# Bucketed attention and a snake MLP on one core: first batch pair by pair, alpha folded into the weights, one form of mask rows

## The chip, the cores and the metric

The kernel runs on 1 core of one Trainium2 chip. The metric is device time in microseconds (us) of one execution. A run is listed as slow when it is more than 1.5% above the fastest of the same kernel, and as fast otherwise. A ratio in this text is the mean time of one kernel's fast runs over the mean of the other's fast runs of the same rounds, so it is not quite the ratio of the medians that stand beside it. The rounds ran on different chips of the same kind; where kernels of different rounds are compared, the ratios are the safer figures.

Engines: PE multiplies matrices (PEld is its loading of weights), DVE and ACT work on vectors, POOL is the general engine, SP issues most of the DMA transfers.

## The reference, cut to what matters

```python
# q, k, v: (4, 8, 768, 64) = batch, heads, positions, head size; proj: (64, 6)
q_bits = (q @ proj > 0); k_bits = (k @ proj > 0)         # 6 bits: a bucket number
mask   = q_bucket[..., :, None] == k_bucket[..., None, :]
scores = where(mask, q @ k.T / 8, -1e9)
attn   = softmax(scores) @ v                             # -> x: (3072, 512)
h = x @ w_in                                             # expand: 512 -> 2048
s = sin(alpha * h)
g = h + s * s / (alpha + 1e-9)
out = g @ w_out                                          # contract: 2048 -> 512
```

## The kernel before

The kernel plans its own order. Every piece of work is an operation with an engine, an assumed duration, dependencies, a priority and buffers; a list scheduler in Python runs once while the kernel is built and fixes the order of each engine. On the chip every engine then runs its own list strictly in order. An assumed duration that is wrong therefore costs a wait, not a new order.

The unit of attention is one pair of heads, one half (384 positions) of the queries: 6 score steps, each followed by an exponential, sums for the denominator, the product with v, ln and exp for the reciprocal. One batch has 8 units.

```python
# the mask: rows of +-32 below the 64 rows of q and k make non-matching buckets vanish in the exponential
NROW = 2 * NB; KR = D + 2 * NROW                          # 64 + 24 = 88 rows
nc.vector.tensor_scalar(out=bits[:, 0, :],      in0=z, ..., op0=ALU.is_gt, op1=ALU.mult)
nc.vector.tensor_scalar(out=bits[64:128, 1, :], in0=z[64:128], ...)          # a second form for k
# 4 row transfers for each pair, 24 rows each
# [cut]
# weights straight from HBM to bf16 by the transfer
nc.gpsimd.dma_start(out=win[p][:, cs], in_=moe_w_in[128*p:128*p+128, cs])
# [cut] expand: two 384-wide Sin with a per-partition scale, two 384-wide fused adds
for i in range(2):
    nc.scalar.activation(out=s[:, i, :], in_=two(hh, "pair")[i][:, 0:HS], func=AF.Sin, scale=alpha[:, 2*s_+i:2*s_+i+1])
for i in range(2):
    nc.vector.scalar_tensor_tensor(out=g[:, F, :], in0=s2[:, i, :], scalar=inva[:, F:F+1],
                                   in1=two(hh, "pair")[i][:, 0:HS], op0=ALU.mult, op1=ALU.add)
# [cut] batch 0 in two groups: the first halves of all four pairs, expand, the second halves, expand
groups = [(0, [(p, 0) for p in range(NPAIR)], [0]), (0, [(p, 1) for p in range(NPAIR)], [1])]
groups += [(b, [(p, c) for p in range(NPAIR) for c in range(2)], [0, 1]) for b in range(1, B)]
```

The contraction of one group is what fills PE during the attention of the next group.

The softmax here doesn't subtract the row's maximum and nothing guards it: scores larger than these inputs give would overflow.

## Time and profile before

| | before |
|---|---|
| median (fast runs) | 381.2 us |
| span in the profile | 379.2 us |
| first score | 18.0 us |
| attention of batch 0 / its expand phases | 36 + 27 us / 14 + 19 us |
| attention of batches 1, 2, 3 | 55, 55, 45 us |
| expand phases of batches 1, 2 | 28, 29 us |

Two lines of the page of the kernel before: PE's busy time with its share of the span, and the clock that PE was granted in 40 equal slices of the span (in tenths of full speed, 9 is 90% or more).

```profile
PE 327.4 (86%) x1914; PEld 153.9 (41%) x1936; DVE 285.7 (75%) x494; ACT 280.3 (74%) x430; POOL 79.7 (21%) x107
...
PEclk9996799699999999699999999999999999999899
```

The windows view of the kernel before, cut at the loads of ACT's function table, which part attention (exponentials) from expand phases (Sin): start and end, length, then the busy time of each engine with its number of instructions, the granted clock, the busy share of DMA and GB/s.

```profile
core 0: us, PE busy (x) PEld busy (x) DVE busy (x) ACT busy (x) POOL busy (x), PEclk, DMA share, GB/s
0.00:18.00 18.00, 10.37 (x63) 6.58 (x64) 10.67 (x49) 3.43 (x4) 8.56 (x21) 1.00 0.91 219
18.00:53.90 35.90, 28.37 (x171) 11.72 (x171) 25.07 (x46) 26.93 (x42) 15.14 (x25) 0.86 0.98 155
53.90:68.30 14.40, 10.98 (x65) 6.20 (x64) 13.31 (x23) 14.12 (x23) 3.70 (x4) 1.00 0.22 35
68.30:95.00 26.70, 25.56 (x146) 10.30 (x148) 20.45 (x32) 22.33 (x34) 5.29 (x6) 0.87 0.46 76
95.00:113.60 18.60, 16.48 (x98) 8.42 (x101) 16.06 (x28) 13.78 (x21) 5.42 (x6) 1.00 0.20 42
113.60:168.20 54.60, 47.42 (x280) 19.88 (x283) 44.05 (x65) 44.12 (x67) 13.95 (x15) 0.94 0.53 90
168.20:196.30 28.10, 24.11 (x146) 13.03 (x146) 26.29 (x46) 24.82 (x42) 5.42 (x6) 1.00 0.19 30
196.30:251.30 55.00, 50.22 (x309) 22.15 (x314) 43.14 (x62) 44.01 (x65) 13.70 (x15) 1.00 0.52 94
251.30:280.50 29.20, 26.28 (x156) 14.48 (x157) 28.61 (x51) 24.13 (x41) 4.17 (x5) 1.00 0.15 30
280.50:325.90 45.40, 44.76 (x278) 19.74 (x282) 31.10 (x54) 39.45 (x61) 4.35 (x4) 1.00 0.22 54
325.90:379.20 53.30, 42.87 (x216) 21.43 (x215) 26.93 (x49) 23.13 (x40) 0.00 (x0) 0.97 0.09 32
```

The second line is the first four units of batch 0, the third an expand phase, and so on in turn; the last is batch 3's expand and the final contraction. PE is nearly full in batch 3's attention (44.76 of 45.40 us), which has no next batch to prepare. Expand phases have DVE busy for 86% to 98% of the time (the last line, which holds the contraction too, aside). DMA is full until 54 us.

Groups of instructions of the kernel before (line, engine, operation, shapes, count, busy us, mean ns, then idle time before them):

```profile
L467 DVE TENSOR_TENSOR sum<-sum,E 128x768 bf16<-128x768 bf16 x64 | 40.1, 626 | 5.3 <-ACT E L457 1.5
L543 ACT ACTIVATE s<-pp,alpha 128x384 bf16<-128x384 f32 x108 | 55.6, 579 | 13.6 <-PE pp L537 13.3
L559 DVE SCALAR_TENSOR_TENSOR g<-s,inva,pp 128x384 bf16<-128x384 bf16 x108 | 59.8, 606 | 1.1 <-ACT s L550 0.2
```

The first line is a group of the adds for the denominators. One step of an expand phase took two Sin of 579 ns on ACT and two adds of 606 ns on DVE.

### The profile page before, as it was taken

The page shows a single profiled execution, that of the slowest core. Times are in us where ns is not written, and L with a number is a line of the kernel's source. Part 1 is how long each engine was busy: PE and PEld are TensorE (multiplying, and loading weights), DVE is VectorE, ACT ScalarE, POOL GpSimd, SP SyncE. Part 2 cuts the span into 40 slices and gives each one's busy share as a digit, 9 for nine tenths or more (in the row PEclk, how much of TensorE's full clock was granted, in tenths as well). Part 3 has the DMA queues.
Part 4 walks back from the last instruction along what each step waited for, and adds up shares of the span by engine and source line. Part 5 has one row for each costly group of instructions (what it writes and reads, how often), then busy time and mean ns, then how long its engine had stood idle before and what let it go on. Part 6 is the DMA issues. An engine that isn't in the chain of part 4 may idle for free.

```text
span 379.2 us, 5493 instructions
## 1 busy us (share of the span) xinstructions
PE 327.4 (86%) x1914; PEld 153.9 (41%) x1936; DVE 285.7 (75%) x494; ACT 280.3 (74%) x430; POOL 79.7 (21%) x107
## 2 busy tenths in 40 slices
PE   3787787899799997787899889997999999897895
PEld 3442244243354332244444333443544344454342
DVE  4797479679895888978977987899986956599121
ACT  1357899798778888599799784898789899798000
POOL 5475210204500315402300540332000300000000
PEclk9996799699999999699999999999999999999899
DMA  8859990155306277351033724651024101100022
GB/s 208 208 81 182 214 148 14 21 91 101 75 7 112 66 110 116 53 98 24 0 59 69 131 51 73 136 111 21 17 51 89 45 3 45 40 0 0 2 83 83
DMA packets 94859, 28.80 MB, mean 76 GB/s; under 512 B 79664, under 2 KB 90736, under 8 KB 94832
## 3 DMA queue, kind: packets, MB, share of 16 engines
q1 hardware_dynamic: 86560, 21.11, 26.8%
q0 software_dynamic: 7680, 7.34, 13.0%
q8 instruction: 15, 0.25, 0.3%
q10 hardware_dynamic: 592, 0.00, 0.1%
q14 instruction: 12, 0.10, 0.1%
HBM read 27.27 MB, written 6.29 MB: 89 GB/s over the span
## 4 chain that ended last, share of the span: by engine, by line
PE 47%; DVE 23%; ACT 12%; DMA 7%; issue 7%; SPq 3%; DVEq 0%
PE pb L580 16%; PE pp L453 10%; PE pp L537 10%; PE pp L491 7%; DVE g L559 5%; ACT E L457 5%; DVE sum L467 5%; DVE F L337 3%; DMA tok<-in_k_dram 3%; DVE s L552 3%; ACT s L543 2%; DMA tok<-in_q_dram 2%; DMA QK<-bits 2%; SPq L327 2%; PE pb L355 2%
## 5 line engine op out<-in xcount | busy, mean ns | idle before, releaser
L457 ACT ACTIVATE E<-pp 128x768 bf16<-128x768 f32 x192 | 148.9, 812 | 28.1 <-PE pp L453 27.1
L453 PE MATMUL pp<-QK 88*128 88x384 bf16 x384 | 92.3, 341 | 12.2 <-ACT E L457 8.0
L580 PE MATMUL pb<-wout,g 128*128 128x512 bf16 x362 | 96.0, 386 | 7.6 <-DVE g L559 3.4
L398 POOL CAST QK<-F 64x768 bf16<-64x768 f32 (+1 forms) x63 | 53.9, 860 | 205.4 <-DVE F L337 194.1
L537 PE MATMUL pp<-xt,win 128*128 128x384 bf16 x432 | 74.6, 326 | 10.4 <-DVE g L559 9.5
L537 PEld LDWEIGHTS <-win 128*128 128x128 bf16 x512 | 49.8, 98 | 49.1 <-issue 16.3
L467 DVE TENSOR_TENSOR sum<-E 128x768 bf16<-128x768 bf16 x64 | 38.3, 604 | 37.5 <-ACT E L457 37.3
L543 ACT ACTIVATE s<-pp,alpha 128x384 bf16<-128x384 f32 x108 | 55.6, 579 | 13.6 <-PE pp L537 13.3
L559 DVE SCALAR_TENSOR_TENSOR g<-s,inva,pp 128x384 bf16<-128x384 bf16 x108 | 59.8, 606 | 1.1 <-ACT s L550 0.2
L453 PEld LDWEIGHTS <-QK 88*128 88x128 bf16 x384 | 33.0, 100 | 64.5 <-issue 41.0
L580 PEld LDWEIGHTS <-g 128*128 128x128 bf16 x384 | 37.0, 99 | 49.7 <-issue 16.4
L491 PE MATMUL pp<-E,V 128*64 128x385 bf16 x384 | 46.3, 350 | 4.3 <-DVE xt L510 3.7
L467 DVE TENSOR_TENSOR sum<-sum,E 128x768 bf16<-128x768 bf16 x64 | 40.1, 626 | 5.3 <-ACT E L457 1.5
L337 DVE STREAM_TRANSPOSE F<-tok 128x768 f32<-128x768 f32 x24 | 37.7, 1572 | 1.3 <-DMA tok<-in_q_dram 1.2
L591 DVE COPY osb<-pb 128x512 f32<-128x512 f32 x20 | 13.7, 688 | 25.1 <-PE pb L580 25.0
L491 PEld LDWEIGHTS <-V 128*64 128x64 bf16 x384 | 17.6, 112 | 31.1 <-issue 26.9
L552 DVE TENSOR_TENSOR s<-s 128x768 bf16<-128x768 bf16 x40 | 22.3, 567 | 6.4 <-ACT s L543 6.2
L504 ACT ACTIVATE ln<-pp,epsb 128x384 f32<-128x384 f32 x32 | 18.6, 582 | 11.0 <-PE pp L496 10.5
L510 DVE SCALAR_TENSOR_TENSOR xt<-pp,ln 128x384 bf16<-128x384 f32 x32 | 19.7, 616 | 1.5 <-ACT ln L507 1.3
L467 DVE TENSOR_TENSOR sum<-sum 128x768 bf16<-128x768 bf16 x32 | 20.3, 633 | 0.7
L550 ACT ACTIVATE s<-s 128x768 bf16<-128x768 bf16 x22 | 18.4, 843 | 0.6
L507 ACT ACTIVATE ln<-ln 128x384 f32<-128x384 f32 x32 | 16.8, 523 | 0.0
(49 smaller groups left out, 185.2 us busy)
## 6 DMA issues: line engine op xcount, KB each, us to landing
out_dram<-osb SPq DMA_DIRECT2D x24, 256.0 KB
tok<-in_q_dram SPq DMA_DIRECT2D x48, 96.0 KB
tok<-in_k_dram SPq DMA_DIRECT2D x48, 96.0 KB
V<-in_v_dram POOLq DMA_DIRECT2D x16, 192.0 KB, 3.8
QK<-bits SPq DMA_DIRECT2D x60, 36.0 KB
win<-in_moe_w_in_dram POOLq DMA_DIRECT2D x8, 256.0 KB, 7.3
wout<-in_moe_w_out_dram POOLq DMA_DIRECT2D x8, 256.0 KB, 12.2
tok<-in_q_dram SPq DMA_DIRECT2D x4, 384.0 KB
```

The source lines that it names most:

```text
L337: nc.vector.transpose(out=fh[0].slots["F"][:, ti, :].rearrange("p (j i a) -> p a j i", j=NJ, a=4), in_=hold_t.slots["tok"].rearrange("p (t ...
L398: nc.gpsimd.tensor_copy(out=d_, in_=s_)
L453: nc.tensor.matmul(out=o.slots["pair"][:, h, 0:HS], lhsT=qk[0:KR, 1, h, 128 * j:128 * j + 128], rhs=qk[0:KR, 0, h, c * HS:(c + 1) * HS], s ...
L457: ex = P.op("ACT", 0.695, lambda o, e, sc=sc, j=j: nc.scalar.activation(out=eh.slots["E"][:, j, :, 0:HS], in_=sc.slots["pair"][:, :, 0:HS] ...
L467: o = P.op("DVE", 0.47, lambda o, e: nc.vector.tensor_tensor(out=dst(), in0=a(), in1=b_(), op=ALU.add), deps=deps + [sh], prio=10 + ui * 1 ...
L491: nc.tensor.matmul(out=nd[D * h:D * h + D, 0, 0:HS + 1], lhsT=vt[:, h, jmap(b, j), :], rhs=et[:, j, h, 0:HS + 1], start=(j == 0), stop=(j ...
L510: xe = P.op("DVE", 0.6, lambda o, e: nc.vector.scalar_tensor_tensor(out=xt_hold[(b, c)].slots["xt"][:, p, :], in0=v0.slots["nd"][:, 0, 0:H ...
L537: nc.tensor.matmul(out=two(o, "pair")[i][:, 0:HS], lhsT=win[p][:, 128 * F:128 * F + 128], rhs=xt[:, p, :], start=(p == 0), stop=(p == NPT ...
L543: nc.scalar.activation(out=o.slots["s"][:, i, :], in_=two(hh, "pair")[i][:, 0:HS], func=AF.Sin, scale=alpha[:, 2 * s_ + i:2 * s_ + i + 1])
L552: (nc.gpsimd if e == "POOL" else nc.vector).tensor_tensor(out=o.slots["s2"], in0=x, in1=x, op=ALU.mult)
L559: nc.vector.scalar_tensor_tensor(out=gh.slots["g"][:, F, :], in0=sq.slots["s2"][:, i, :], scalar=inva[:, F:F + 1], in1=two(hh, "pair")[i][ ...
L580: nc.tensor.matmul(out=acc, lhsT=g_hold[(b, c)].slots["g"][:, F, 128 * tb:128 * tb + 128], rhs=wout[:, F, :], start=(F == 0), stop=(F == N ...
```

## The change

Intent: in batch 0 use each pair for two units in turn, so that only pair 0 has to be ready early, and have one expand phase instead of two. Scale the weights by alpha once (w_in by alpha, w_out by 1/alpha), so that Sin and the add need no per-partition scale and can run 768 wide. Use one 12-row form of the mask rows instead of two, with 8 row transfers instead of 4 for the 12 late pairs (those of batches 1 to 3). Order the preparation of a pair by the unit that needs it.

```diff
-    KR = D + 2 * NROW
+    KR = D + NROW
-SET_SIN = 10
+SET_SIN = 9                                  # with set 10 a second load followed each entry to Sin
-    groups = [(0, [(p, 0) for p in range(NPAIR)], [0]), (0, [(p, 1) for p in range(NPAIR)], [1])]
-    groups += [(b, [...], [0, 1]) for b in range(1, B)]
+    groups = [(b, [(p, c) for p in range(NPAIR) for c in range(2)], [0, 1]) for b in range(B)]
     # preparation: priority by due unit, and started one pair earlier
+        due = 4.0 if pid == 0 else 4.5 if pid == 1 else 10 + (2 * pid - LEAD) * 1e-3
-        pid = (ui + 5) // 2
+        pid = (ui + 7) // 2
     # late pairs: one bits instruction, 8 row transfers of 12 rows (before: two, and 4 of 24)
-            nc.vector.tensor_scalar(out=o.slots["bits"][64:128, 1, :], ...)
+                r = 64 * t + 32 * c + NROW * h
+                return qk[D:KR, t, h, HS * c:HS * c + HS], b_[r:r + NROW, 0, :]
     # weights: float32 into lent g buffers, then folded
+                    out=win[p][:, cs], in0=ld.slots["stage"], in1=abc[:, cs], op=ALU.mult)      # POOL or DVE, 8 times
+                out=wout[:, 2*F2:2*F2+2, :], in0=..., in1=inva[...].to_broadcast(...), op=ALU.mult)  # POOL, 8 times
     # first of the five adds of a unit on POOL
-        a0 = add(Z(0), E(0), E(1), [exps[0], exps[1]])
+        a0 = add(Z(0), E(0), E(1), [exps[0], exps[1]], ("POOL",))
     # expand
-                for i in range(2): nc.scalar.activation(..., func=AF.Sin, scale=alpha[...])
+                    nc.scalar.activation(out=o.slots["s"], in_=hh.slots["pair"][:, :, 0:HS], func=AF.Sin)
-                for i in range(2): nc.vector.scalar_tensor_tensor(...)
+                    nc.vector.tensor_tensor(out=gt[:, 2*s_:2*s_+2, :], in0=s2, in1=hh.slots["pair"][:, :, 0:HS], op=ALU.add)
     # [cut] early hash in two row groups; assumed durations closer to measured ones; mask rows of pair 0 by transfers
```

## The prediction

> **What bounds the kernel now.** The page shows PE busy 327 of 379.2 us (86%), DVE 286, ACT 280. PE work at its sustained rates in the chain of waits (expand 24 matmuls in 4.06 us, contract 4 in 0.86, values 6 in 0.68, scores 4 in 0.76) adds up, with hash and transposes, to an estimated 310 us: some 70 us are PE gaps. By stage (the timeline's table loads divide them):
> - start to first score: 18 us, DMA busy 91%;
> - four units of batch 0: 36 us, 9 per unit though ACT needs only 6 (six exponentials of 0.81, ln 0.58, exp 0.52). PE clock 0.86, DMA 98%; the chain holds a 6.8 us wait for mask rows. All four pairs are needed at once.
> - expand phases: 14.4 + 18.6 (batch 0), 28.1, 29.2, 24: DVE 90% or more busy, PE needs 21.6 per batch;
> - attention of batches 1 and 2: 55 each, batch 3 (no preparation of a next batch) 45.4, PE 99% busy;
> - last contraction: 29, PE-bound.
>
> **What the change does.**
> 1. Batch 0 goes pair by pair: 8 units, then one expand phase of 16 steps. One round of table switches goes, and each entry to Sin needs one load, not two (the trace shows 1.28 + 1.28 us): 15 loads become 9. The Trainium skill ("ScalarE: Activation LUTs", What ACT_TABLE_LOAD costs) also gives about 1283 ns; the trace agrees. Rows and loads of pair 1 are due two units later and no longer gate. Against this: batch 0's attention has no contraction to fill PE, so it is ACT/DVE-bound.
> 2. Alpha in the weights: Sin in one 768-wide instruction (estimate 0.8 instead of 2x0.55), the add likewise (0.9 instead of 1.06 to 1.2). Per step DVE+ACT falls from 2.8 to 2.3 us; expand becomes PE-bound: 28 to 23 us.
> 3. Cost: 16 folds of 1024 float32 columns (estimate 1.1 us on DVE, 2 on POOL) inside batch 0's attention.
> 4. 12 mask rows in one form: second bits instruction (0.69 x 12 late pairs) gone, early hash 1.52 to perhaps 0.8 us. 8 row transfers instead of 4; SP has room.
> 5. First of five adds of each unit to POOL: 32 x 0.6 us off DVE, 1.46 each on POOL. The Trainium skill ("GPSIMD Engine Reference", Specifications) says that POOL and DVE share SBUF interfaces; the trace agrees: adds have a median of 0.56 us but up to 1.17 beside POOL casts. Half of the saving may go back.
>
> **Predicted stages** (estimates): first score 17 to 18 (the new PE order puts transposes up to pair 3's q ahead of it, behind a saturated DMA), attention 0 about 55, expand 0 24: batch 0 ends near 97 instead of 113.6, with 10 us of contraction still owed. Batches 1 and 2: 53+23.5 and 52+23.5 instead of 83 and 84. Batch 3: 46+23 instead of 69.5; tail 29. Sum 350 us, PE about 91% busy.
>
> **Time: 350 us, range 338 to 364.** Faster by over 2%: 0.94; within 2%: 0.05; slower: 0.01.
>
> **What would show it.** Units of batch 0 near 6.5 us; expand phases 22 to 24 us with PE over 90%; nine table loads; DVE busy down to about 265, POOL up to 150, ACT down to 260; PE busy unchanged within 10; DVE adds' mean above 0.65. First score not before 16.
>
> **What would make it wrong.** Slower: POOL folds late, so batch 0's contraction or second half of expand (whose buffers are lent to staging) waits; POOL adds delaying the denominators; lower PE clock in denser stages; SP late with rows. Faster: first score at 13 to 14, or attention dropping to batch 3's 45 us.

## More of the kernel before

The timeline of SP's queue in the kernel before (start, us that the issuing took, transfers):

```profile
19.76 13.74 SPq L237 DMA_DIRECT2D QK<-bits  x12
33.60 8.73 SPq L327 DMA_DIRECT2D tok<-in_q_dram  x4
42.43 11.04 SPq L327 DMA_DIRECT2D tok<-in_k_dram  x4
```

SP issued without a pause from 19.8 to 56.2 us: mask rows of batch 0, then loads of q and k (tok) for batch 1.

## The result, and the profile after

The changed kernel takes 368.88 us (median of 4 runs, 367.44 to 370.42) against 382.14 (380.92 to 383.62) in the same rounds: ratio 0.9652, 95% interval 0.9589 to 0.9715. It is faster, but by 13 us and not by the 32 that were predicted, and it lies outside the range of 338 to 364.

The same two lines of the page, of the kernel after:

```profile
PE 331.3 (90%) x1916; PEld 159.3 (44%) x1936; DVE 273.2 (75%) x384; ACT 258.7 (71%) x369; POOL 145.8 (40%) x144
...
PEclk9996555657999999989999999969999999999999
```

PE has 90% of the span and nearly the same busy time as before. But the granted clock is at five and six tenths in slices 4 to 9, that is from 27 to 82 us: a busy PE that runs at half speed.

The windows of the kernel after, again cut at the table loads, with the same columns:

```profile
0.00:16.90 16.90, 9.31 (x74) 6.40 (x74) 11.04 (x38) 4.36 (x5) 10.38 (x25) 1.00 0.99 240
16.90:87.60 70.70, 61.65 (x287) 21.18 (x288) 61.41 (x71) 48.90 (x72) 48.51 (x45) 0.61 0.82 182
87.60:116.40 28.80, 26.66 (x157) 14.64 (x158) 25.73 (x31) 20.38 (x26) 13.51 (x10) 1.00 0.21 44
116.40:168.00 51.60, 49.48 (x310) 23.06 (x312) 39.84 (x53) 44.23 (x67) 25.16 (x23) 0.97 0.55 99
168.00:192.30 24.30, 23.63 (x149) 13.23 (x150) 23.15 (x32) 20.78 (x27) 4.29 (x5) 1.00 0.19 31
192.30:245.60 53.30, 50.25 (x309) 23.71 (x311) 40.30 (x54) 43.63 (x66) 25.86 (x23) 0.96 0.48 90
245.60:273.00 27.40, 25.96 (x157) 14.32 (x157) 23.68 (x33) 19.48 (x27) 6.39 (x6) 0.96 0.20 32
273.00:317.90 44.90, 43.45 (x274) 21.77 (x275) 23.34 (x42) 38.85 (x59) 10.27 (x7) 1.00 0.10 36
317.90:366.10 48.20, 40.87 (x216) 21.02 (x215) 24.71 (x37) 18.08 (x26) 1.47 (x1) 1.00 0.09 33
```

| stage | predicted | measured |
|---|---|---|
| first score | 17 to 18 us | 16.9 us |
| attention of batch 0 | 55 us | 70.7 us |
| expand 0 | 24 us | 28.8 us |
| attention and expand, batch 1 | 53 + 23.5 us | 51.6 + 24.3 us |
| attention and expand, batch 2 | 52 + 23.5 us | 53.3 + 27.4 us |
| attention, batch 3 | 46 us | 44.9 us |
| expand 3 and last contraction | 52 us | 48.2 us |

Most of the miss is one stage: the attention of batch 0, 16 us too long. There the mean clock is 0.61, and DVE and PE are both busy for 61 of 71 us.

The groups that answer to those shown of before, and the adds on POOL:

```profile
L483 POOL TENSOR_TENSOR sum<-E 128x768 bf16<-128x768 bf16 x32 | 48.4, 1514 | 107.7 <-ACT E L473 93.2
L561 ACT ACTIVATE s<-pp 128x768 bf16<-128x768 f32 x53 | 42.5, 807 | 22.3 <-PE pp L554 19.7
L483 DVE TENSOR_TENSOR sum<-sum,E 128x768 bf16<-128x768 bf16 x64 | 48.9, 765 | 4.4 <-ACT E L473 1.8
L579 DVE TENSOR_TENSOR g<-s,pp 128x768 bf16<-128x768 bf16 x53 | 48.8, 947 | 3.1 <-PE pp L554 0.6
```

Sin now takes 807 ns for two blocks that took 1158, and the add 947 for what took 1212. The adds on POOL take 1514 ns each. The DVE adds shown have a mean of 765 ns where they had 626; their median is 558 ns in both kernels, so some adds are much longer and most are not.

The timeline of PE in batch 0's attention, kernel after (start, us, engine, line, operation, count; the last column is idle time before it and what ended it):

```profile
53.29 1.46 PE L469 MATMUL pp<-QK 76*128 76x384 bf16 x4
55.01 0.80 PE L469 MATMUL pp<-QK 76*128 76x384 bf16 x2 [0.26 <-ACT E L473]
56.12 0.80 PE L469 MATMUL pp<-QK 76*128 76x384 bf16 x2 [0.31 <-ACT E L473]
```

Two score matmuls take 0.80 us; at full clock they take 0.48, as an experiment below shows. PE is slow, and still waits for ACT now and then, but only briefly: from 24 to 63 us its timeline shows no gap over 0.63 us, and in the low clock from 33 to 63 us none over 0.31.

The timeline of SP's queue, kernel after: how long it took to issue transfers.

```profile
15.18 13.68 SPq L250 DMA_DIRECT2D QK<-bits  x12
...
44.27 8.05 SPq L337 DMA_DIRECT2D tok<-in_k_dram  x4
52.42 6.52 SPq L337 DMA_DIRECT2D tok<-in_q_dram  x4
59.13 8.13 SPq L250 DMA_DIRECT2D QK<-bits  x8
...
71.12 6.41 SPq L250 DMA_DIRECT2D QK<-bits  x8
```

SP issues from 15 to 90 us with only short pauses: 8 row transfers take 6.4 to 8.1 us, 4 token loads (tok, the loads of q and k) up to 8 us. DMA is full until about 62 us.

One line of DVE's and one of POOL's timeline, kernel after, in expand 0. First DVE:

```profile
101.25 3.54 DVE L572 TENSOR_TENSOR s<-s 128x768 bf16<-128x768 bf16 x2
```

Then POOL:

```profile
100.32 4.06 POOL L443 TENSOR_TENSOR wout<-g,inva 128x1024 bf16<-128x1024 f32 x2
```

Two squares took 3.54 us beside two folds on POOL; in the kernel before, such a square has a mean of 567 ns. The profile counts the extra time as busy time of DVE.

The folds that fell to DVE, kernel after (minimum, median and maximum in ns):

```profile
L435 DVE TENSOR_TENSOR win<-g,g x6: 1209/1213/3354, 30.2 to 48.3; 128x1024 bf16<-128x1024 f32 x6
```

A seventh fold on DVE took 2483 ns; the eighth of w_in and all eight of w_out ran on POOL.

### The profile page after: what moved, and what is told of

It is laid out like the page before. It is cut to its first block, busy times and chain, and to the rows that moved or that the text cites. A ratio compares the mean times of both kernels' runs of the same rounds, so it can differ in the third digit from the quotient of the medians.

```text
span 366.1 us, 5576 instructions
## 1 busy us (share of the span) xinstructions
PE 331.3 (90%) x1916; PEld 159.3 (44%) x1936; DVE 273.2 (75%) x384; ACT 258.7 (71%) x369; POOL 145.8 (40%) x144
## 4 chain that ended last, share of the span: by engine, by line
PE 58%; DVE 15%; ACT 13%; issue 5%; DMA 5%; SPq 2%; POOL 0%; DVEq 0%; ACTq 0%
PE pb L602 16%; PE pp L469 13%; PE pp L554 12%; PE pp L510 10%; ACT E L473 8%; DVE sum L483 4%; DVE g L579 3%; DVE s L572 3%; PE pb L554 2%; DMA tok<-in_k_dram 2%; DMA tok<-in_q_dram 2%; PE pb L358 2%; PE pp L507 2%; ACT ln L524 1%; ACT ln L521 1%
## 5 line engine op out<-in xcount | busy, mean ns | idle before, releaser
L469 PE MATMUL pp<-QK 76*128 76x384 bf16 x384 | 101.3, 366 | 11.0 <-ACT E L473 9.5
L483 POOL TENSOR_TENSOR sum<-E 128x768 bf16<-128x768 bf16 x32 | 48.4, 1514 | 107.7 <-ACT E L473 93.2
L469 PEld LDWEIGHTS <-QK 76*128 76x128 bf16 x384 | 36.2, 104 | 69.7 <-issue 42.5
L405 POOL CAST QK<-F 64x768 bf16<-64x768 f32 x52 | 48.2, 927 | 34.6 <-DVE F L347 30.1
L561 ACT ACTIVATE s<-pp 128x768 bf16<-128x768 f32 x53 | 42.5, 807 | 22.3 <-PE pp L554 19.7
L483 DVE TENSOR_TENSOR sum<-sum,E 128x768 bf16<-128x768 bf16 x64 | 48.9, 765 | 4.4 <-ACT E L473 1.8
L579 DVE TENSOR_TENSOR g<-s,pp 128x768 bf16<-128x768 bf16 x53 | 48.8, 947 | 3.1 <-PE pp L554 0.6
L483 DVE TENSOR_TENSOR sum<-E 128x768 bf16<-128x768 bf16 x32 | 23.5, 733 | 20.9 <-ACT E L473 18.6
L521 ACT ACTIVATE ln<-pp,epsb 128x384 f32<-128x384 f32 x32 | 18.6, 580 | 27.6 <-PE pp L507 27.6
L510 PEld LDWEIGHTS <-V 128*64 128x64 bf16 x384 | 21.3, 120 | 28.9 <-issue 21.8
L572 DVE TENSOR_TENSOR s<-s 128x768 bf16<-128x768 bf16 x37 | 25.3, 685 | 7.1 <-ACT s L561 5.9
```

What stands on the lines that cost most here:

```text
L405: nc.gpsimd.tensor_copy(out=d_, in_=s_)
L469: nc.tensor.matmul(out=o.slots["pair"][:, h, 0:HS], lhsT=qk[0:KR, 1, h, 128 * j:128 * j + 128], rhs=qk[0:KR, 0, h, c * HS:(c + 1) * HS], s ...
L483: o = P.op(eng, {"DVE": 0.57, "POOL": 1.62}, lambda o, e: (nc.vector if e == "DVE" else nc.gpsimd).tensor_tensor(out=dst(), in0=a(), in1=b ...
L510: nc.tensor.matmul(out=nd[D * h:D * h + D, 0, 0:HS + 1], lhsT=vt[:, h, jmap(b, j), :], rhs=et[:, j, h, 0:HS + 1], start=(j == 0), stop=(j ...
L521: ln = P.op("ACT", 0.47, lambda o, e: nc.scalar.activation(out=o.slots["ln"], in_=v0.slots["nd"][:, 1, 0:HS], func=AF.Ln, bias=epsb[:, :]) ...
L561: nc.scalar.activation(out=o.slots["s"], in_=hh.slots["pair"][:, :, 0:HS], func=AF.Sin)
```

## The experiments

Theories for the 16 us, as they stood at the start. **A**: PE has gaps in batch 0's attention, because no contraction is there to fill it, so its clock is halved, and that makes the stage long. **B**: the clock is lowered by the load of all engines and DMA at once. **C**: DVE with the folds bounds the stage, whatever the clock. Two more came up after the first runs. **D**: SP's queue and the full DMA bound it. **E**: several of these are limits of nearly equal length.

All experiments start from the changed kernel. `fill`, `nofold`, `rows4`, `dveadd` and `unfold` change what is emitted, not the plan: the order of the other instructions stays that of the changed kernel. Where a result is wrong, it says so.

### fill4 and fill8: give PE more to do

```diff
                                      rhs=qk[0:KR, 0, h, c * HS:(c + 1) * HS], start=True, stop=True)
+                if ui < 8:
+                    for i in range(4):               # fill8: range(8), fill2: range(2)
+                        nc.tensor.matmul(out=o.slots["pair"][:, i % 2, HS:HS + 128], lhsT=fil[:, :],
+                                         rhs=fil[:, :], start=True, stop=True)   # read by nobody
```

> The changed kernel, with 4 extra matmuls of 128 columns (into unused PSUM columns of the same buffer) behind each of the 48 score steps of batch 0; every other instruction and the order stay. Their results are read by nobody. In the changed kernel batch 0's attention runs at a granted PE clock of 0.50 from 33 to 87 us. Theory A (the clock falls because PE has gaps there, no contraction being there to fill it): the clock in 30 to 85 us rises to over 0.9, scores x4 take about 0.82 instead of 1.46 us, batch 0's attention ends 6 to 12 us earlier, total 357 to 363 us although PE gets about 10 us more work. Theory B (the clock is lowered because the load of all engines and DMA is high there): more PE work keeps 0.50 or lower and costs up to 20 us more: 375 to 390 us. Theory C (DVE with the folds bounds the stage, the clock is beside the point): clock may rise, time stays 366 to 371.

> As the run with 4 extra matmuls, but 8 behind each score step. Theory A: clock 1.0 throughout the stage; total as with 4 or up to 5 us more, for PE then is filled: 357 to 366 us. Theory B: 390 to 410 us. Theory C: 368 to 374 us.

Measured: fill4 367.60 us (ratio 0.9671 to before), fill8 366.57 (0.9631). The clock rises as theory A says. The windows view, 30 to 60 us, of the kernel after and then of fill4:

```profile
30.00:60.00 30.00, 26.62 (x104) 8.47 (x104) 26.18 (x30) 22.10 (x33) 18.43 (x19) 0.55 1.15 228
```

```profile
30.00:60.00 30.00, 25.23 (x240) 15.25 (x239) 27.28 (x34) 25.30 (x38) 20.24 (x22) 1.00 1.08 211
```

More work on PE brought the clock from 0.55 to 1.00. That refutes B: load had not halved the clock, too little work on PE had. Whether the short gaps count there, or that the matmuls of attention are narrow (76 rows, or 64 columns) and the extra ones 128 by 128, the runs do not separate. The time hardly moved, as theory C had said for this run. The second half of A, that the clock by itself made the stage long, fell: attention 0 ended at 87.9 and 86.7 us instead of 87.6. The extra matmuls take time of their own, 19 us of PE in fill4, and could have hidden a gain; but doubling them in fill8 did not lengthen the stage, so with folds and row transfers in place PE was not what held it. The chain of waits (each step followed back to what released it) of fill4, 18 to 84 us, agrees: SP's token loads lead with 18.3%, DVE's adds follow with 11.5%. Others held the stage at nearly the same length.

### nofold: empty the folds

```diff
-  get=lambda o: (o.slots["stage"], moe_w_in[...])
+  get=lambda o: (win[p][:, cs], moe_w_in[...])          # cast by the transfer, as before
-  out=win[p][:, cs], in0=ld.slots["stage"], in1=abc[:, cs]
+  out=win[p][:, cs.start:cs.start+2], in0=win[p][:, cs.start:cs.start+2], in1=abc[:, cs.start:cs.start+2]
   # the same for w_out; result wrong on purpose
```

> The changed kernel, with the alpha folds emptied: the weights go straight from HBM to bf16 (as in the kernel before), and each of the 16 fold instructions is cut to 2 columns. Order of PE and ACT identical. Result wrong on purpose (weights not scaled). Theory A (PE gaps lower the clock): clock in batch 0's attention stays near 0.5, attention 0 gets at most 3 us shorter; expand 0 gets about 4 us shorter since the POOL folds no longer block the squares on DVE; total 361 to 367 us. Theory B (load lowers the clock): the clock rises to about 0.8 and the total falls to 350 to 358. Theory C (folds on DVE bound the stage): total 352 to 358 us with the clock still at 0.5.

Measured: 363.92 us (0.9555), attention 0 ends at 82.2. Expand 0 gained only 0.7 us (26.9 instead of 27.6 between the table loads), not the 4 that I expected. Window 30 to 60 us of nofold:

```profile
30.00:60.00 30.00, 26.36 (x103) 8.23 (x101) 15.64 (x28) 22.30 (x33) 15.87 (x18) 0.55 1.06 154
```

DVE fell from 26.18 to 15.64 us in this window, and the clock stayed at 0.55. So removing load does not bring the clock back (B again falls), and taking ten microseconds off DVE gives five. That is more than the 3 us that theory A allowed the stage, and the total is not as low as C forecast. The edit relieves the DMA too, for the weights now land as bf16 (154 GB/s in this window instead of 228), so what is called the folds from here on is the folding with its float32 loads; the two were not separated.

### dveadd: the POOL adds back on DVE

```diff
-  (nc.vector if e == "DVE" else nc.gpsimd).tensor_tensor(
+  nc.vector.tensor_tensor(
```

> The changed kernel, with all adds of the denominators on DVE again (32 adds of 1.5 us on POOL become adds of 0.55 to 0.6 us on DVE), same order otherwise. If POOL's adds cost more by blocking DVE than they take off it: 358 to 366 us. If they help as intended: 372 to 380. My own prediction said that half the saving goes back, so about neutral to slightly worse: 368 to 373 us. The clock in batch 0 should not change by over 0.1 under theory A.

Measured: 369.54 us (0.9724, interval 0.9647 to 0.9800; verdict of record: unclear). Two of the four runs are listed as slow; the fast ones took 364.57 and 368.37 us, the changed kernel 367.44 to 370.42. The mean of these two would give 0.963, so the recorded ratio is not to be leaned on. The difference is not clear of noise. Adds on POOL are about neutral.

### fill8_nofold, rows4, all3

```diff
   # rows4: 4 row transfers for a late pair, both halves from the first half's bits; wrong on purpose
-                r = 64 * t + 32 * c + NROW * h
-                return qk[D:KR, t, h, HS * c:HS * c + HS], b_[r:r + NROW, 0, :]
+                r = 64 * t + NROW * h
+                return (None, None) if c else (qk[D:KR, t, h, :].rearrange("p (c x) -> p c x", c=2),
+                                               b_[r:r + NROW, 0:1, :].to_broadcast([NROW, 2, HS]))
```

> Both at once: 8 extra matmuls behind each score step of batch 0 and the folds emptied (wrong result on purpose). Filling alone brought the clock to 1.00 but only 1 to 2 us of time, emptied folds alone 5 us with the clock still at 0.5 in 33 to 60 us. Theory E (clock and folds are two limits of about equal length, one on PE and one on DVE, so that either alone hides the other): attention 0 ends near 70 us, total 346 to 354 us. Theory D (SP's queue, which is issuing transfers without a pause from 15 to 92 us, and the saturated DMA behind it set the pace, by way of PE's in-order wait for batch 1's hash): attention 0 ends at 79 to 84 us, total 358 to 364.

> The changed kernel, with 4 mask-row transfers for each of the 12 late pairs instead of 8, each writing both halves from the first half's bits (wrong result on purpose), otherwise the same order. Theory D: SP's queue gets about 3 us shorter per pair, some 10 us in batch 0; attention 0 ends 2 to 6 us earlier: 360 to 366 us. Theory E (clock and folds): under 1.5 us, 366 to 370.

> All three at once: 8 extra matmuls per score step of batch 0, folds emptied, 4 row transfers per late pair (wrong result on purpose). If clock, folds and SP are three limits of similar length: attention 0 ends at 66 to 71 us (my prediction was 73), total 345 to 352 us. If it is no better than the best pair of them, the limit is elsewhere (DMA bandwidth, POOL): 358 to 364.

Measured: fill8_nofold 363.71 us (0.9546), rows4 364.75 (0.9586), all3 362.72 (0.9532). Attention 0 ends at 87.5, 88.8 and 84.9. So rows4 reached the total that theory D gave, but not by its path: attention 0 ended 1.2 us later than in the changed kernel, and the 4 us came in later stages. In all3 this looked as if theory E were wrong. The chain of waits showed why not: eight extra matmuls behind each score took 24% of the chain in 17 to 82 us, so the filling itself had become the limit. The dose was too high.

### two_groups: undo "pair by pair" alone

```diff
-    groups = [(b, [(p, c) for p in range(NPAIR) for c in range(2)], [0, 1]) for b in range(B)]
+    groups = [(0, [(p, c) for p in range(NPAIR)], [c]) for c in range(2)]
+    groups += [(b, [(p, c) for p in range(NPAIR) for c in range(2)], [0, 1]) for b in range(1, B)]
```

> The changed kernel with batch 0 in two groups again (first all four pairs' first halves, expand, then the second halves), all else kept. This undoes the first part of the change alone. If pair by pair is worth what I predicted (a table round, no waits for all pairs at once), the total is 374 to 380 us. If the low clock eats it up because no contraction fills PE, the two are level: 364 to 371 us, with a clock of 0.5 only in the first group and at the start of the second.

Measured: 375.01 us (0.9839). The medians differ by 6 us from the changed kernel, so this part is worth about 6 of the change's 13 us. The scheduler made a new order for this one, and what the other 7 us came from was not tested.

This run also limits what can be said of the clock. Its first group has no contraction beside it, like that of the kernel before, yet its clock is 0.65 (17 to 58 us) where the kernel before had 0.86 (18 to 54 us). Its second group, with a contraction, has 0.90 (75 to 108 us). So the lost contraction is not the only thing that lowered the clock in batch 0. What else in the change did it (the score matmuls have 76 rows now instead of 88, for one) was not tested.

### fill2, and the three reliefs with a smaller dose

> 2 extra matmuls of 128 columns behind each score step of batch 0 instead of 4 or 8. With 8, the extra work itself took 24% of the chain in batch 0's attention, so that it gave back what the full clock won. If the clock needs only a little less idling: clock over 0.9 in 30 to 85 us, attention 0 ends at 79 to 84, total 360 to 364 us. If 2 are too few: clock 0.5 to 0.7, total 367 to 371. If folds and DMA hold the stage whatever the clock: clock up, total 366 to 369.

> As the run with all three, but 4 extra matmuls per score step instead of 8 (wrong result on purpose). With 8 the chain there alternated between PE (extra matmuls in it) and ACT, with PE busy 95%. Three limits of similar length (clock, folds on DVE, SP and DMA): attention 0 ends at 68 to 75 us, total 346 to 355. If DMA bandwidth itself holds the stage: 80 us and more, total 358 to 363.

Measured: fill2 368.75 us (0.9655), with a clock of 0.72 in 30 to 60 us: two extra matmuls are not enough to hold the clock. With four extra matmuls and the other two reliefs (wrong on purpose): **353.70 us (0.9272, interval 0.9189 to 0.9355)**, and attention 0 ends at 76.6 us, a little later than the 68 to 75 expected. The window of that stage:

```profile
17.00:76.60 59.60, 50.54 (x485) 29.24 (x484) 46.91 (x72) 49.11 (x71) 39.70 (x47) 1.00 0.95 152
```

The stage has shrunk from 70.7 to 59.6 us at full clock. PE's timeline in it (L477 are the extra matmuls):

```profile
44.81 0.48 PE L472 MATMUL pp<-QK 76*128 76x384 bf16 x2 [0.40 <-ACT E L480]
45.13 0.39 PE L477 MATMUL pp<-fil 128*128 128x128 bf16 x4
45.45 0.68 PE L517 MATMUL pp<-E,V 128*64 128x385 bf16 x6
```

The score pair takes 0.48 instead of 0.80 us, and the extra matmuls run in the gap while ACT works.

### The pairs

> Clock and folds relieved, 8 row transfers kept (wrong result on purpose). If those two are the cause and SP's transfers are not: 353 to 356 us, as with all three. If SP is a third limit: 357 to 361, attention 0 ends at 79 to 82 us.

> Clock and row transfers relieved, folds kept (wrong result on purpose). If DVE with the folds is a limit by itself once the clock is full: 363 to 367 us, attention 0 ends at 84 to 88. If the folds count only together with the low clock: 355 to 359.

> Folds emptied and 4 row transfers, no extra matmuls (wrong result on purpose). If the low PE clock is a limit of its own: clock near 0.5 in 33 to 60 us, attention 0 ends at 80 to 84 us, total 359 to 364. If the clock is beside the point: 352 to 356 us, as with the extra matmuls.

The edits are those above, two at a time. All eight combinations, each compared with the kernel before:

| filled by 4 | folds emptied | 4 transfers | median us | ratio | attention 0 ends at | clock, 30 to 60 us |
|---|---|---|---|---|---|---|
| | | | 368.88 | 0.9652 | 87.6 | 0.55 |
| x | | | 367.60 | 0.9671 | 87.9 | 1.00 |
| | x | | 363.92 | 0.9555 | 82.2 | 0.55 |
| | | x | 364.75 | 0.9586 | 88.8 | 0.61 |
| x | x | | 361.80 | 0.9467 | 81.9 | 1.00 |
| x | | x | 365.21 | 0.9556 | 85.9 | 0.89 |
| | x | x | 360.84 | 0.9526 | 83.4 | 0.56 |
| x | x | x | 353.70 | 0.9272 | 76.6 | 1.00 |

The low clock alone costs nothing that shows (368.88 against 367.60). With the other two gone it costs 7 us (360.84 against 353.70), and that is what is left after the extra matmuls have been paid for. The row transfers cost 8 us once the others are gone (361.80 against 353.70), the folds 11.5 (365.21 against 353.70). By the ratios, times 381.5 us, the three are about 10, 7 and 11 us, and the interval of the last line touches none of the others. This is theory E.

What took over is to be read in the chain of waits of batch 0's attention: the shares of the chain by engine and line. First the kernel after, 18 to 84 us:

```profile
by line: PE pp L469 27.5%; ACT E L473 18.0%; PE pp L510 17.5%; DVE sum L483 9.9%; issue 4.1%; ACT ln L524 3.9%; DMA tok<-in_q_dram 3.8%; PE pb L358 3.4%; PE pp L507 3.0%; DVE QK L409 2.5%; DVE F L327 1.5%; SPq L250 1.3%; DVE bits L380 1.1%;
```

PE at half clock alternates with ACT. Then fill4_nofold in the same window, where clock and folds are out of the way:

```profile
by line: ACT E L479 16.8%; PE pp L471 15.2%; SPq L251 11.8%; PE pp L516 8.8%; DMA tok<-in_k_dram 8.6%; PE pp L476 8.0%; issue 7.5%; SPq L339 6.6%; DMA QK<-bits 2.7%; DVE bits L382 2.7%; ACT ln L530 2.5%; PE pp L311 2.3%; ACT ln L527 1.6%; D
```

Now SP's issuing (L251 rows, L339 token loads) and the token transfers themselves are 27% of the chain. PE's list holds the hash of batch 1's first pairs ahead of the last work of batch 0, and the hash needs those tokens; in fill4, PE waits 4.0 us there. Then all three, 18 to 76 us:

```profile
by line: ACT E L480 26.2%; PE pp L472 23.7%; PE pp L517 13.6%; PE pp L477 11.5%; issue 6.5%; ACT ln L531 4.4%; ACT ln L528 3.6%; PE pb L361 2.7%; PE pp L514 1.4%; PE pb L370 1.4%; PE pp L370 1.4%; DVE bits L383 1.1%; PE pp L312 1.1%; DVE xt
```

No SP and no DMA in the leading entries: ACT's exponentials with PE in between. The extra matmuls (L477) are 11.5% of this chain, so the price of holding the clock is still in it.

### fill2_late: prepare one pair later

```diff
-        pid = (ui + 7) // 2
+        pid = (ui + 5) // 2          # with fill2
```

> 2 extra matmuls per score step, and the preparation of each late pair starts one pair later (two and a half pairs ahead as in the kernel before, instead of three and a half), which takes transposes, hashes, loads and row transfers of one pair out of batch 0's attention. If the queue of SP and the saturated DMA hold batch 0: attention 0 ends 3 to 8 us earlier than with 2 extra matmuls alone, total 355 to 362 us. If not: same as that run or up to 3 us slower, for the pairs come late in batch 1.

Measured: 380.73 us (0.9957), attention 0 ends at 89.6, and batch 1's attention takes 59.7 us between the table loads instead of 52.9. This edit makes a new plan, so it is not a clean test of D. It does show that the earlier start of the preparation is needed.

### unfold: what folding is worth, and versions with a right result

```diff
   # unfold: straight loads, folds cut to 2 columns of scratch, Sin and add in two instructions as before
+  for i in range(2): nc.scalar.activation(..., func=AF.Sin, scale=alpha[:, 2*s_+i:2*s_+i+1])
+  for i in range(2): nc.vector.scalar_tensor_tensor(..., scalar=inva[:, F:F+1], ..., op0=ALU.mult, op1=ALU.add)
   # rows4ok: late pairs hash like early ones, into two banks, so that one transfer serves both halves
+  lhsT=pn[D*h:D*h+D, NB*t:NB*t+NROW], rhs=fh[0].slots["F"][D*h:D*h+D, t, c*HS:(c+1)*HS],
+  tile_position=(D*h, 32*(2*t+h))                            # out: bank c, rows 32*(2*t+h)
```

> The changed kernel with alpha taken out of the weights: weights loaded straight to bf16, the folds cut to 2 columns written to scratch, Sin in two instructions with a per-partition scale and the add in two with inva, as in the kernel before (result right); order as in the changed kernel. What the fold is worth net: the four expand phases should grow by about 4 us each, attention 0 shrink by 5: 374 to 382 us by my prediction's sizes. If folding hardly pays: 366 to 372.

> Right result: alpha outside of the weights as in the kernel before (Sin in two instructions), and 4 extra matmuls per score step of batch 0. If the low clock and the folds are two limits side by side: attention 0 ends at 77 to 82 us, total 357 to 362 us, faster than the changed kernel (368.9) though each of the two alone left it where it was (367.6 and 370.2). If not additive: 365 to 370.

> Right result: alpha outside of the weights and 4 row transfers by the two-bank hash, no extra matmuls. With the extra matmuls it took 362.9 us. If the clock is a limit of its own: 366 to 372. If it is beside the point: 361 to 364.

> As the run before, and the late pairs hash like the early ones, into two banks, so that 4 row transfers suffice (right result). The bits instruction doubles its columns (about 1.1 instead of 0.67 us), and the order of all engines is planned anew. If fewer transfers help and the new order is as good: 353 to 359 us. If the two banks make the hash wait for the contraction: 360 to 368.

All four give right results. Measured: unfold 370.23 us (0.9604, interval 0.9499 to 0.9710; two of its four runs are listed as slow, the fast ones took 365.14 and 368.65), unfold_fill4 369.66 (0.9667; its profiled run was slow and is left out of the ratio; the 357 to 362 expected was missed), unfold_rows4ok 366.77 (0.9654), unfold_fill4_rows4ok **362.94 (0.9494, interval 0.9412 to 0.9576)**. The last has the full clock in 30 to 60 us and ends attention 0 at 76.9 us. It beats both kernels; its interval does not touch that of the changed kernel. Without the extra matmuls, unfold_rows4ok, it is 3.8 us slower, so the clock counts in a kernel with a right result too. It does not reach 353.70: from Sin to the end of the expand phase its batch 1 takes 28.3 us between the table loads, against 23.0 in the changed kernel. In unfold, with the order of the changed kernel, it takes 25.4, so the two-instruction Sin and add make 2.4 us of the difference; the other 2.9 come with the two-bank hash and the new order.

## Why the prediction was right or wrong

**Right: most stages and counts.** First score at 16.9 us, POOL 146 us, ACT 259, PE busy 331 (unchanged within 10), DVE adds slower than 0.65 us on the mean: as predicted. So were batch 1 and the attention of batches 2 and 3, within 2 us. There were eight table loads (1.28 us each) where nine were predicted, and DVE was 273 instead of 265. That PE's busy time came out right is partly luck: the score matmuls count 101.3 us instead of 92.3 because more of them ran at half clock.

**Wrong: "attention 0 about 55".** It took 70.7 us, 8.8 for each unit instead of near 6.5. The prediction read from the absence of a contraction that the stage is "ACT/DVE-bound", and priced it at full clock. This is the step that failed; the runs showed three limits side by side. (1) The clock: the trace has 0.50 for most of 33 to 87 us, and more work on PE brought 1.00. The prediction did list a lower clock as a risk, but "in denser stages"; it is a stage with too little PE work. It also listed the 0.86 of the first group before, and did not carry it over. (2) The folds were under-costed, at "1.1 us on DVE": five of the seven folds on DVE took 1.2 us, but the other two 2.5 and 3.4, and DVE's adds beside POOL's folds grew too, up to 2.2 us. (3) "8 row transfers instead of 4; SP has room" was false in this stage: SP issues from 15 to 90 us almost without a pause, and the trace of the kernel before already showed none from 19.8 to 56.2. It has room only as a mean over the kernel. Removing any one of the three gives 1 to 5 us, all three give 15 (11 of them before attention 0 ends): 353.7 us, close to the 350 predicted. Even then the stage takes 59.6 us and not 55, with the extra matmuls in it; that the total comes so near is helped by the last stretch, which took 48 us instead of 52. I had costed the stage by its average engine and by one limit.

**Half right: "expand becomes PE-bound: 28 to 23 us".** Sin and the add shrank to 807 and 947 ns, near the 0.8 and 0.9 estimated, and expand 1 took 24.3 us with PE at 97%. Expand 0 and 2 took 28.8 and 27.4. The whole fold, though, is worth nothing that shows: unfold is 1.3 us slower by medians, but two of its runs are slow ones, and by the ratios of fast runs it is 0.5% faster (0.9604 against 0.9652), within noise. What the folds cost in batch 0 (attention 0 ends 4.7 us earlier without them) comes back in later stages (expand 1 is 2.4 us and the last stretch 4 us shorter with them).

**Right in kind: adds on POOL.** "Half of the saving may go back": as far as can be told, all of it did (369.54 against 368.88, with slow runs in the first). The Trainium skill ("SBUF — State Buffer", SBUF: two separate sides) says more than the page that I named: the shared pair of ports is an exclusive lock, held for a whole instruction. This trace agrees in kind: two squares took 3.54 us on DVE beside 4.06 us of POOL folds, and ended within 0.5 us of them.

**Confirmed in sign: pair by pair.** Undoing it costs 6 us, in a plan that is new as a whole.

The Trainium skill ("TensorE: Matmul & The Clock Gate", Part 1: The HAM clock gate) states that PE's clock is halved after an idle window and restored after about 3.4 us of sustained work. Had I used it for the stage whose filler the change takes away, I might have priced that stage at two clocks. The trace agrees on the two levels (0.50 and 1.00). It does not show an idle window before the drop: no gap in PE's timeline from 24 to 63 us is over 0.63 us, so by the idle window alone the drop would not have been expected.

## What to carry to other kernels

When a change leaves a stage with little work for PE, price the stage at half its clock too, and look whether a few useless matmuls in the gaps hold the clock; too many become the limit themselves. Check a serial issuing queue in the stage where it is needed, not over the whole span. When single removals each give little, remove them together before calling any of them harmless: here 1 + 5 + 4 us apart became 15 together.

## What the Trainium skill lacked or had wrong

- "TensorE: Matmul & The Clock Gate" gives no measure of how busy PE must be, only sustained or idle. Here two extra matmuls of 128 columns per score step left a mean clock of 0.72 in 30 to 60 us, four gave 1.00. And between 36 and 63 us PE counts as busy for 2.4 to 3.0 of every 3 us while the clock stays at 0.50, with no gap over 0.31 us, so the busy time of the profile does not tell the clock; what does was not found. (The busy time is itself longer at half clock.)
- "SBUF — State Buffer" has the lock but no figure for DVE adds beside POOL work. Here a bf16 add of 128x768 on DVE has a median of 0.56 us and reaches 2.25 beside a POOL fold of 2.2 us.
- "DMA: Bandwidth & Descriptors" has no figure that I found for what a full DMA does to the issuing queue. Here 4 token loads took SP 2.7 us to issue when the busy share of DMA was 0.41 and up to 8.05 us when it was 1.23; row transfers took about 0.8 us each even at a share of 0.05.
